# A planned order for a residual quantizer: hand-over margins and a rank offset per stage and tile

## The chip, the cores and the metric

The kernel runs on one core of one Trainium2 chip. The metric is the device time of an execution in microseconds, and the number of a kernel is the median over several executions. Before the change it is 731.85 us (six runs, 729.74 to 734.48).

## The reference

The input `x` is (2, 16000, 512) in bf16: two sequences of 16000 time steps with 512 channels. A depthwise convolution over three time steps, then SiLU, gives `z`. Four codebooks of eight vectors each then quantize it one after the other, and a second depthwise convolution makes the output.

```
z = silu(sum_i xp[:, i:i+T, :] * dw_enc[i])        # K = 3 taps
res = z; q = 0
for s in range(4):
    d2  = |res|^2 - 2 res . cb[s] + |cb[s]|^2
    idx = argmin(d2);  sel = cb[s][idx]
    q += sel;  res -= sel
y = sum_i qp[:, i:i+T, :] * dw_dec[i]              # K = 3 taps
```

The output `y` has the shape and type of `x`. The choice at each level hangs on the residual of the level before, so the levels of one row can't run side by side; different rows can.

## The kernel before

**Tiles.** The rows of the two sequences are cut into 18 tiles of G blocks of 128 rows: 6, 8, then fourteen of 16, then 8 and 6. The tensors of a tile have channels on the partitions, four blocks of 128 channels (KT = 4), so that x is loaded by transposing DMAs, one per block of rows, on SyncE (SP).

**Stages of a tile.** Each has a name in the planner's tables and these engines:

- `load`, `pad`: transposing loads into XT (two buffers), 16 to 18 for a large tile; edges by GpSimd or by two more loads.
- `taps`: three products by the encoder's weights and two sums, on half of the channels at a time (h = 0, 1), into Z. Mostly VectorE (DVE); a product may go to ScalarE (ACT).
- `exp`, `plus1`, `recip`, `gate`: SiLU as z / (1 + exp(-z)). The exponential and the reciprocal are on ACT, with a table load at each change between them; "plus one" is on DVE or ACT; the product is on DVE.
- `score0`: matmuls on TensorE (PE) of Z with itself and with the codebooks, into PSUM, half a tile at a time; DVE collects them.
- `decide`: for levels 0 to 2 a chain of small DVE instructions makes a one-hot choice. Between levels, PE transposes the one-hot (line 639), a copy on ACT or DVE brings it to SBUF (lines 643, 644), PE makes a correction from it (line 649), and DVE adds that to the scores (lines 617, 622). The scores of levels 1 and 2 thus don't need the updated residual.
- `win0`: PE transposes the one-hots of three levels (line 672), one copy brings them to OHW (line 678).
- `resid`: 24 updates per tile (three levels, two parities, four channel blocks). PE forms minus the chosen vectors in two PSUM banks (line 701). On DVE the update is an addition to Z (line 709). On ACT it is a copy (line 707), for which PE first adds Z itself by a product with the identity (line 700): four matmuls instead of two.
- `score3`, `decide3`, `win3`: the same for the last level.
- `back`: the decoder's convolution as matmuls of the one-hot windows with prepared weights (lines 758 to 762), copied by ACT to YB (line 766) and stored by SP (line 789).

**PSUM.** Four pairs of banks (PS); a step that `take`s banks holds them until the step that `free`s them has run.

**What sets the order.** All steps are entered in a list with their engine (or a choice of two), a cost in microseconds, the tensors read and written, and a key (stage, tile, place within the stage). `Plan.order` walks this list: it keeps for each engine the time at which it is free, and for each step the time at which its inputs are there; again and again it takes the step that could start first, and among equals the one with the lowest rank. The rank is the tile's number plus an offset and a slope of the stage (`WHEN`), each given for the first three tiles, the middle, and the last three. After a step, its users become ready at its end plus `LATENCY` of the engine (0.2 us for PE, 0.15 for DVE, 0.22 for ACT), or `AGAIN` on the same engine. `SHARE` decides which engine takes a residual update, `QUOTA` how many updates each may have under way, `SLACK` how much later ACT may end a movable step than DVE would. Where PE would stand idle, `order` puts filler matmuls (line 809, identity times MSK) in front of the next step; `product` models PE's granted clock. The steps are then issued in this order, which fixes each engine's instruction stream; at run time an engine takes its own stream in order and waits where an input isn't there.

Of the kernel before, what the change touches and what calls it, by code (L numbers as in the profile page):

```python
# [12 lines left out]
ACT = mybir.ActivationFunctionType  # L13
# [3 lines left out]
class Plan:  # L17
# [9 lines left out]
    SPAN, BUSY = 3.413, 0.5  # L27
    GATE = {"resid": (1.0, 2.0), "back": (1.0, 2.0), "win0": (0.6, 1.5), "win3": (0.6, 1.5), "score0": (0.25, 1.4), "score3": (0.25, 1.4)}

    def __init__(self, pairs, edges, share, slack, quota, when):  # L30
        self.steps, self.writer, self.readers = [], {}, {}
        self.pairs, self.edges, self.share, self.slack, self.quota, self.when = pairs, edges, share, slack, quota, when

    def add(self, engine, cost, key, fn, reads=(), writes=(), take=None, free=None, hold=None, tail=0.0, after=(), dest=None, box=None, mm=0):
        n = len(self.steps)
# [18 lines left out]

    def rank(self, s):
        w = self.when[s["k"][0]][self.part(s)]
        return w[0] + s["k"][1] + w[1] * s["k"][2]

    def product(self, t, c, share, half):

# [14 lines left out]
    def order(self):  # L75
# [8 lines left out]
        at = [0.0] * len(steps)  # L84
        clock = {e: 0.0 for e in self.LATENCY}
        waiting = {e: [] for e in clock}
        held = {e: 0 for e in clock}
        banks = [0.0] * (2 * self.pairs)
# [6 lines left out]
        def cost(s, e):  # L95
            return s["c"][e] if isinstance(s["c"], dict) else s["c"]

        def place(kind, t):
            if kind == "A":
                return min((max(banks[j], banks[j + 1], t), 0, j) for j in range(0, 2 * self.pairs, 2))  # L100
            return min((max(banks[j], t), -max(banks[j ^ 1], t), j) for j in range(2 * self.pairs))

        def load(d, t):
            return max(clock[d] - t, 0.0) + held[d] + sum(cost(steps[m], d) for m in waiting[d]
                                                        if at[m] <= t + 1.0 and (d == "DVE" or not isinstance(steps[m]["e"], tuple)))

        def many(s, dest):
            return s["mm"][dest] if isinstance(s["mm"], dict) else s["mm"]

        def late(m, t, c):  # L110

            return max(0.0, fetched - (t + c * (self.CHUNK - run) / m)) if run + m > self.CHUNK else 0.0

        def look(s, e):

            t = max(at[s["n"]], clock[e])
            if s["take"]:
                dest = s["dest"]
                if dest == "ANY":
                    full = [d for d in ("ACT", "DVE") if held[d] >= self.quota[d]]  # L120
                    if len(full) == 2:
                        return inf, None
                    if full:
                        dest = "ACT" if full[0] == "DVE" else "DVE"
                    else:
                        dest = "DVE" if load("DVE", t) + self.share[self.part(s)] < load("ACT", t) else "ACT"
                elif dest and held[dest] >= self.quota[dest]:
                    return inf, None
                kind = s["take"][0]
                t = place(kind[dest] if isinstance(kind, dict) else kind, t)[0]  # L130
                return t + late(many(s, dest), t, cost(s, dest) if s["dest"] == "ANY" else s["c"]), dest
            if isinstance(s["e"], tuple) and e == "ACT" and t + s["c"]["ACT"] > max(at[s["n"]], clock["DVE"]) + s["c"]["DVE"] + self.slack[self.part(s)]:
                return inf, None
            if s["mm"]:
                t += late(s["mm"], t, s["c"])
            return t, None

        def open_(n):
            e = steps[n]["e"]
            for e in e if isinstance(e, tuple) else (e,) if e else ():  # L140
                waiting[e].append(n)

        for s in steps:
            if not left[s["n"]]:
                open_(s["n"])
        while len(out) < len(steps):
            (t, dest), _, n, e = min(((look(steps[n], e), rank[n], n, e) for e, names in waiting.items() for n in names),
                                     key=lambda q: (q[0][0], q[1], q[2], q[3]))
            assert t < inf
            s = steps[n]  # L150
            for w in waiting.values():
                if n in w:
                    w.remove(n)
            c = cost(s, dest if s["take"] and s["dest"] == "ANY" else e)
            s["fill"] = None
            if s["mm"] and s["k"][0] != "setup":
                j = min(range(2 * self.pairs), key=lambda j: (banks[j], j))
                since = max(clock["PE"], banks[j])
                k = 0
                while t - clock["PE"] > self.AFTER and since + self.REST + self.FILL * (1 if self.full else 2) < t:  # L160
                    since = self.product(since, self.FILL, 1.0, 2.0)
                    k += 1
                if k > 0:
                    s["fill"] = (j, k)
                    run += k
                    if run > self.CHUNK:
                        run -= self.CHUNK
                        fetched = t + self.FETCH
            if s["take"]:
                kind, box = s["take"]  # L170
                kind = kind[dest] if isinstance(kind, dict) else kind
                j = place(kind, t)[2]
                box["banks"] = [j, j + 1] if kind == "A" else [j]
                for j in box["banks"]:
                    banks[j] = inf
                box["dest"] = dest
                if s["dest"] == "ANY":
                    steps[n + 1]["e"] = dest
                if dest:
                    held[dest] += 1  # L180
            elif s["box"] is not None:
                s["box"]["dest"] = e
            if s["hold"] and table != s["hold"]:
                table = s["hold"]
                c += self.TABLE
            if s["mm"]:
                m = many(s, dest)
                c = self.product(t, c, *self.GATE.get(s["k"][0], (0.5, 1.5))) - t
                run += m
                if run > self.CHUNK:  # L190
                    run -= self.CHUNK
                    fetched = t + c * (m - run) / m + self.FETCH
            s["t"], s["d"], s["on"] = t, c, e
            clock[e] = t + c
            self.busy[e] += c
            end = t + c + s["tail"]
            if s["free"]:
                if s["free"]["dest"]:
                    held[s["free"]["dest"]] -= 1
                for j in s["free"]["banks"]:  # L200
                    banks[j] = end + self.LATENCY[e]
            out.append(s)
            for u in users[n]:
                ue = steps[u]["e"]
                at[u] = max(at[u], t + c + self.AGAIN[e] if ue == e else end + self.LATENCY[e])
                left[u] -= 1
                if not left[u]:
                    open_(u)
# [5 lines left out]
def kernel(  # L214
# [27 lines left out]
    PAIR = 1  # L242
    NX, NE, NZ, NOH, NY = 2, 3, 4, 4, 4
    NA = 4
    SHARE = (19.5, 1.71, -1.34)
    SLACK = (0.8, -4.83, -5.72)
    QUOTA = {"ACT": 4, "DVE": 4}
    WHEN = {"setup": ((-0.05, 1.675), (0.613, 1.016), (0.464, 0.931)), "load": ((-2.074, 0.741), (-2.063, 0.601), (-2.58, 0.741)),
            "pad": ((-1.343, 0.11), (-1.736, 0.115), (-2.291, 0.134)), "taps": ((0.284, 0.643), (-0.413, 0.648), (0.441, 1.172)),
            "exp": ((0.672, 0.139), (0.624, 0.043), (0.853, 0)), "plus1": ((1.287, 0.521), (0.349, 0.234), (0.268, 0.646)),  # L250
            "recip": ((0.542, 0.819), (0.469, 0.213), (1.361, 0.627)), "gate": ((-0.104, 0.712), (0.552, 0.521), (1.523, 0.809)),
            "score0": ((-0.134, 0), (0.889, 0), (-0.19, 0)), "decide": ((1.83, 0.266), (-0.088, 0.293), (0.366, 0.69)),
            "win0": ((2.039, 0), (2.077, 0), (2.756, 0)), "resid": ((1.585, 0.742), (1.683, 0.632), (1.826, 0.993)),
            "score3": ((2.285, 1.086), (2.738, 0.327), (2.939, 1.624)), "decide3": ((1.327, 0.17), (2.815, 0.429), (3.624, 0.724)),
            "win3": ((3.135, 0.143), (3.003, 1.197), (2.818, 0.209)), "back": ((2.723, 0.576), (3.156, 1.159), (4.372, 0.628))}
    assert B == len(SIZES) and T >= GM * P and GM <= 16

    xf = x.flatten_outer_dims()
# [7 lines left out]
    tiles = []  # L266
    for b, sizes in enumerate(SIZES):
        done = 0
        for g in sizes:
            r = g * P  # L270
            t0 = max(0, min(done - 2, T - r))
            end = T if t0 + r >= T else t0 + r - 2
# [49 lines left out]
    CBN = {(s, u): sb([P, D], BF16, f"CBN{s}_{u}") for s in range(3) for u in range(2)}  # L322
    WDEC = [sb([P, D], BF16, f"WDEC{v}") for v in range(4)]

    plan = Plan(NA, (3, len(tiles) - 3), SHARE, SLACK, QUOTA, WHEN)
    add = plan.add

    def ps(box):
# [518 lines left out]
```

## Time and profile before

| | |
|---|---|
| median of six runs | 731.85 us |
| profiled execution, its own time | 730.6 us |
| its span, first to last instruction | 728.8 us |
| VectorE busy | 674.9 us (93%) |
| ScalarE busy | 658.4 us (90%) |
| TensorE busy with matmuls | 581.0 us (80%) |
| weight loads busy | 288.0 us (40%) |
| mean granted TensorE clock | 0.97 |

The rows with the largest busy time, with the mean duration of one instruction:

| line, engine, what | count | mean |
|---|---|---|
| 707 ACT, residual update, 1024 columns | 234 | 1.029 us |
| 709 DVE, residual update, 1024 columns | 102 | 1.213 us |
| 766 ACT, output copy, 1024 columns | 126 | 1.043 us |
| 537, 549 ACT, exponential and reciprocal, 4096 columns | 28 each | 3.624 us |
| 532 DVE, tap product, 2048 columns | 166 | 0.746 us |
| 364 DVE, sum or product of 4096 columns | 84 | 2.29 us |
| 539 DVE, plus one, 4096 columns | 28 | 1.218 us |

A row of the profile names the line and engine of an instruction and the tensors it writes and reads. A wait "A <- B" means that engine A stood idle before its instruction until B ended. The time of a wait is that of the waiting engine alone; whether it lengthens the kernel depends on whether the engine has other time to spare. PEclk is the granted clock of TensorE as a share of the full one. Durations are of one execution; the runs differ by some tenths of a per cent.

### The profile page before, as it was taken

The page shows a single profiled execution, that of the slowest core. Times are in us where ns is not written, and L with a number is a line of the kernel's source. Part 1 is how long each engine was busy: PE and PEld are TensorE (multiplying, and loading weights), DVE is VectorE, ACT ScalarE, POOL GpSimd, SP SyncE. Part 2 cuts the span into 40 slices and gives each one's busy share as a digit, 9 for nine tenths or more (in the row PEclk, how much of TensorE's full clock was granted, in tenths as well). Part 3 has the DMA queues.
Part 4 walks back from the last instruction along what each step waited for, and adds up shares of the span by engine and source line. Part 5 has one row for each costly group of instructions (what it writes and reads, how often), then busy time and mean ns, then how long its engine had stood idle before and what let it go on. Part 6 is the DMA issues. An engine that isn't in the chain of part 4 may idle for free.

```text
span 728.8 us, 24317 instructions
## 1 busy us (share of the span) xinstructions
PE 581.0 (80%) x10656; PEld 288.0 (40%) x10725; DVE 674.9 (93%) x1258; ACT 658.4 (90%) x583; POOL 11.3 (2%) x35
## 2 busy tenths in 40 slices
PE   4977577887898787778778877877798796889995
PEld 2433233443444443434344343433454342444442
DVE  7779889999999999999998999999999999999993
ACT  5888988599999999899998999999999999999666
POOL 2000000000010000000000000000000010000000
PEclk9999898999999999999998999989999999999999
DMA  6454545433346343645544344452535241302316
GB/s 110 99 96 96 97 109 102 118 80 74 53 128 93 117 75 102 125 94 119 96 132 88 96 118 102 142 90 57 88 119 130 71 136 24 119 2 88 117 32 212
DMA packets 163968, 71.89 MB, mean 99 GB/s; under 512 B 155567, under 2 KB 155599, under 8 KB 163862
## 3 DMA queue, kind: packets, MB, share of 16 engines
q1 hardware_dynamic: 163646, 69.90, 41.4%
q8 instruction: 84, 1.38, 0.8%
q10 hardware_dynamic: 216, 0.43, 0.3%
q14 instruction: 22, 0.18, 0.1%
HBM read 0.43 MB, written 32.77 MB: 46 GB/s over the span
## 4 chain that ended last, share of the span: by engine, by line
DVE 53%; PE 24%; issue 8%; ACT 7%; DMA 3%; SPq 3%; ACTq 0%; DVEq 0%
DVE ZB L709 12%; DVE TB L532 7%; DVE TA L364 7%; DVE ZB L364 7%; PE ps L701 6%; PE ps L700 5%; PE ps L567 5%; DVE TA L532 3%; PE ps L758 3%; DVE EX L539 2%; SPq L493 2%; PE ps L809 2%; DVE OHW L678 2%; ACT YB L766 2%; ACT EX L549 2%
## 5 line engine op out<-in xcount | busy, mean ns | idle before, releaser
L701 PE MATMUL ps<-OHW,CBN 128*128 128x512 bf16 (+1 forms) x768 | 265.1, 382 | 20.0 <-DVE ZB L709 10.6
L707 ACT CAST ZB<-ps 128x1024 bf16<-128x1024 f32 (+2 forms) x296 | 253.7, 932 | 29.7 <-PE ps L701 28.5
L700 PE MATMUL ps<-ZB,IDENT 128*128 128x512 bf16 (+1 forms) x530 | 203.2, 383 | 32.5 <-ACT ZB L707 13.6
L709 DVE TENSOR_TENSOR ZB<-ZB,ps 128x1024 bf16<-128x1024 bf16 (+2 forms) x136 | 142.8, 1062 | 2.2 <-PE ps L701 1.7
L766 ACT CAST YB<-ps 128x1024 bf16<-128x1024 f32 x126 | 121.7, 1043 | 9.9 <-PE ps L758 3.8
L701 PEld LDWEIGHTS <-CBN 128*128 128x128 bf16 x768 | 74.1, 98 | 140.5 <-issue 73.0
L537 ACT ACTIVATE EX<-ZB 128x4096 bf16<-128x4096 bf16 (+2 forms) x36 | 115.1, 3197 | 8.8 <-DVE ZB L364 8.5
L549 ACT ACTIVATE EX<-EX 128x4096 bf16<-128x4096 bf16 (+2 forms) x36 | 114.8, 3195 | 0.2
L567 PEld LDWEIGHTS <-ZB 128*32 128x32 bf16 x8064 | 75.4, 95 | 55.2 <-issue 52.2
L567 PE MATMUL ps<-ZB 128*32 128x64 bf16 x8064 | 87.5, 198 | 8.8 <-issue 5.7
L532 DVE TENSOR_SCALAR TB<-XT,WENC 128x2048 bf16<-128x2048 bf16 (+2 forms) x139 | 92.5, 683 | 0.2
L809 PE MATMUL ps<-MSK,IDENT 128*128 128x512 bf16 x277 | 71.6, 406 | 15.4 <-issue 3.1
L758 PE MATMUL ps<-WDEC,OHW 128*128 128x512 bf16 x219 | 67.4, 383 | 14.7 <-DVE ZB L709 4.8
L700 PEld LDWEIGHTS <-IDENT 128*128 128x128 bf16 x530 | 52.3, 99 | 65.2 <-issue 11.6
L364 DVE TENSOR_TENSOR ZB<-ZB,EX 128x4096 bf16<-128x4096 bf16 (+2 forms) x36 | 72.6, 2019 | 3.7 <-ACT EX L549 3.6
L364 DVE TENSOR_TENSOR TA<-TA,TB 128x4096 bf16<-128x4096 bf16 (+2 forms) x36 | 72.7, 2020 | 1.0 <-ACT TB L531 0.6
L364 DVE TENSOR_TENSOR ZB<-TA,TB 128x4096 bf16<-128x4096 bf16 (+2 forms) x36 | 72.8, 2023 | 0.1
L809 PEld LDWEIGHTS <-IDENT 128*128 128x128 bf16 x294 | 29.1, 102 | 48.1 <-issue 20.6
L532 DVE TENSOR_SCALAR TA<-XT,WENC 128x2048 bf16<-128x2048 bf16 (+2 forms) x70 | 46.7, 687 | 0.9 <-DMA XT<-in_x_dram 0.4
L758 PEld LDWEIGHTS <-OHW 128*128 128x128 bf16 x252 | 22.8, 98 | 41.9 <-issue 19.0
L539 DVE TENSOR_SCALAR EX<-EX 128x4096 bf16<-128x4096 bf16 (+2 forms) x35 | 38.4, 1096 | 0.8 <-ACT EX L537 0.8
L678 DVE COPY OHW<-ps 96x1024 bf16<-96x1024 bf16 (+5 forms) x35 | 22.1, 630 | 10.7 <-PE ps L672 5.6
(100 smaller groups left out, 396.0 us busy)
## 6 DMA issues: line engine op xcount, KB each, us to landing
out_dram<-YB SPq DMA_DIRECT2D x33, 448.0 KB
out_dram<-YB SPq DMA_DIRECT2D x28, 512.0 KB
XT<-in_x_dram SPq DMA_TRANSPOSE x283
out_dram<-YB SPq DMA_DIRECT2D x30, 60.0 KB
out_dram<-YB SPq DMA_DIRECT2D x31, 2.0 KB
out_dram<-YB SPq DMA_DIRECT2D x2, 224.0 KB
YB<-in_dw_dec_dram ACTq DMA_DIRECT2D x1, 384.0 KB
out_dram<-YB SPq DMA_DIRECT2D x1, 384.0 KB
```

The source lines that it names most:

```text
L364: add("DVE", cost, key, lambda: nc.vector.tensor_tensor(out=out, in0=a, in1=b, op=op), reads, writes, **kw)
L532: lambda dst=dst, src=src, w=w: nc.vector.tensor_scalar(out=dst, in0=src, scalar1=w, scalar2=None, op0=ALU.mult),
L537: add("ACT", act(2 * R), ("exp", n, h), lambda: nc.scalar.activation(v(ex), Z, ACT.Exp, scale=-1.0), zt, [("EX", sl), "ACTTAB"], hold="E")
L549: nc.scalar.add_instruction(mybir.InstActivation(name=nc.get_next_instruction_name(), engine=mybir.EngineType.Activation, func=ACT.Reciprocal,
L567: nc.tensor.matmul(o[HB * q:HB * (q + 1), u * ZW:(u + 1) * ZW].rearrange("p (s c) -> p s c", s=2), lhsT=blk, rhs=both, start=False, stop=( ...
L700: nc.tensor.matmul(o, lhsT=IDENT, rhs=zg[:, k0:k0 + nk, :], start=True, stop=False)
L701: nc.tensor.matmul(o, lhsT=CBN[s, u][:, i * P:(i + 1) * P], rhs=W[:, k0:k0 + nk, PADC:PADC + P], start=not on_act, stop=True)
L707: nc.scalar.copy(zg, v)
L709: nc.vector.tensor_tensor(out=zg, in0=zg, in1=v, op=ALU.add)
L758: nc.tensor.matmul(o, lhsT=W[:, k, PADC:PADC + P], rhs=WDEC[u], start=True, stop=not wrap)
L766: add("ACT", act_psum(1024), key, lambda k=k, box=box, Y=Y, k0=k0: nc.scalar.copy(Y[:, 2 * (k - k0):2 * (k - k0) + 2, :].rearrange("p g d ...
L809: nc.tensor.matmul(PS[j // 2][:, 512 * (j % 2):512 * (j % 2) + NMK * ZW], lhsT=IDENT, rhs=MSK.rearrange("p u w -> p (u w)"), start=True, s ...
```

## The change

The planner gets four margins, and every number that steers it is replaced. `MARGIN[0]` (0.11 us) is added where a step of another engine uses what PE made, `MARGIN[1]` (0.10 us) where PE uses what another engine made, `MARGIN[2]` (0.09 us) before a PSUM bank counts as free again, and PE's cost is multiplied by `MARGIN[3]` (0.99). A table `NUDGE` gives for each stage and tile an offset that is added to the rank, and, under "share" and "slack", offsets for the two choices of engine. `SHARE`, `SLACK` and `WHEN` have new values, and DVE may have three updates under way instead of four. No step, cost, latency, buffer or instruction is edited: the kernel computes the same through a different order, with some steps on the other engine and other filler.

```diff
@@ class Plan
-    def __init__(self, pairs, edges, share, slack, quota, when):
+    def __init__(self, pairs, edges, share, slack, quota, margin, when, nudge):
...
     def rank(self, s):
         w = self.when[s["k"][0]][self.part(s)]
-        return w[0] + s["k"][1] + w[1] * s["k"][2]
+        return w[0] + s["k"][1] + w[1] * s["k"][2] + self.more(s["k"][0], s)
+
+    def more(self, name, s):
+        return self.nudge.get(name, (0,) * 99)[s["k"][1]] if s["k"][0] != "setup" and s["k"][1] >= 0 else 0.0
...
-                        dest = "DVE" if load("DVE", t) + self.share[self.part(s)] < load("ACT", t) else "ACT"
+                        dest = "DVE" if load("DVE", t) + self.share[self.part(s)] + self.more("share", s) < load("ACT", t) else "ACT"
...
-            if isinstance(s["e"], tuple) and e == "ACT" and t + s["c"]["ACT"] > max(at[s["n"]], clock["DVE"]) + s["c"]["DVE"] + self.slack[self.part(s)]:
+            if isinstance(s["e"], tuple) and e == "ACT" and t + s["c"]["ACT"] > max(at[s["n"]], clock["DVE"]) + s["c"]["DVE"] + self.slack[self.part(s)] + self.more("slack", s):
...
-                c = self.product(t, c, *self.GATE.get(s["k"][0], (0.5, 1.5))) - t
+                c = self.product(t, c * self.margin[3], *self.GATE.get(s["k"][0], (0.5, 1.5))) - t
...
-                    banks[j] = end + self.LATENCY[e]
+                    banks[j] = end + self.LATENCY[e] + self.margin[2]
...
-                at[u] = max(at[u], t + c + self.AGAIN[e] if ue == e else end + self.LATENCY[e])
+                at[u] = max(at[u], t + c + self.AGAIN[e] if ue == e else end + self.LATENCY[e] + (self.margin[0] if e == "PE" else self.margin[1] if ue == "PE" else 0.0))
@@ kernel
-    SHARE = (19.5, 1.71, -1.34)
-    SLACK = (0.8, -4.83, -5.72)
-    QUOTA = {"ACT": 4, "DVE": 4}
+    SHARE = (17.22, 2.23, -0.62)
+    SLACK = (0.55, -4.13, -4.58)
+    QUOTA = {"ACT": 4, "DVE": 3}
+    MARGIN = (0.11, 0.1, 0.09, 0.99)
-    WHEN = {...
-            "win0": ((2.039, 0), (2.077, 0), (2.756, 0)), "resid": ((1.585, 0.742), (1.683, 0.632), (1.826, 0.993)),
-            "win3": ((3.135, 0.143), (3.003, 1.197), (2.818, 0.209)), "back": ((2.723, 0.576), (3.156, 1.159), (4.372, 0.628))}
+    WHEN = {...
+            "win0": ((1.053, 0.009), (1.534, 0), (2.184, 0.009)), "resid": ((1.521, 0.757), (1.683, 0.63), (1.77, 0.949)),
+            "win3": ((3.13, 0.271), (3.063, 1.197), (3.78, 0.216)), "back": ((2.796, 0.565), (3.449, 1.148), (4.298, 0.724))}
+    NUDGE = {...
+             "gate": (0.01, 0, -0.3, 0, 0.05, 0.12, 0.09, 0, 0, -0.03, 0, 0, 0, 0, -0.5, 0, 0.04, 0.08),
+             "score0": (0, 0, 0, 0, 0.56, 0, 0, 0, 0, -0.01, 0.03, -0.21, 0, 0, 0, 0, 0.04, 0.12),
...
+             "share": (0.4, -2.4, 0, -0.5, 0, 0, 0, 0, 0, 0, 0, 0, 0, 0, -1.5, -0.4, -0.4, -0.9),
+             "slack": (0.1, 0, 0, 0, 1.3, -2.8, 0, 0, 0, 0, 0, 0, 0, 0, 0, 1.4, 4, 1.2)}
```

## The prediction

> **What bounds the kernel now.** I read first the busy shares, then a table by stage, then the waits of VectorE (DVE) and ScalarE (ACT), and last the order of time in one bad stretch. The page's first part:
>
> ```profile
> PE 581.0 (80%) x10656; PEld 288.0 (40%) x10725; DVE 674.9 (93%) x1258; ACT 658.4 (90%) x583; POOL 11.3 (2%) x35
> ```
>
> The span is 728.8 us, so DVE is idle 53.9 us and ACT 70.4 us. Both are close to full and share work: each of the 432 residual updates leaves PSUM through either. Where the idle time lies, from busy time in four stretches (columns: length, then PE, PEld, DVE, ACT, POOL busy):
>
> ```profile
> 0.00:140.00 140.00, 101.46 (x1369) 48.65 (x1382) 117.76 (x257) 108.75 (x135) 3.89 (x29) 0.93 0.52 104
> 140.00:420.00 280.00, 228.00 (x4307) 113.97 (x4335) 269.30 (x451) 269.48 (x211) 4.24 (x4) 0.98 0.45 99
> 420.00:700.00 280.00, 231.97 (x4679) 116.01 (x4702) 272.30 (x513) 261.83 (x216) 3.16 (x2) 0.98 0.35 92
> 700.00:728.80 28.80, 19.54 (x311) 9.33 (x311) 15.58 (x40) 18.29 (x23) 0.00 (x0) 0.96 0.40 134
> ```
>
> DVE is idle 22.2 us in the ramp (first line), 10.7 and 7.7 in the middle, 13.2 in the drain. In the middle DVE and ACT are both 94 to 97% busy, so less work helps only if both are relieved; idle time is at most what a new order can win. Who ends those waits (columns: total us, times, longest):
>
> ```profile
> DVE OHW L678 <- PE ps L672: 5.6, 4, 2.3
> DVE rr L601 <- PE ps L567: 5.1, 2, 2.8
> DVE rr L725 <- PE ps L567: 4.6, 7, 1.6
> DVE OHW L678 <- PE ps L567: 4.2, 4, 1.8
> DVE ZB L364 <- ACT EX L549: 3.6, 3, 2.4
> DVE OT L644 <- PE ps L567: 2.5, 3, 1.2
> DVE PR L622 <- PE ps L649: 2.4, 3, 1.6
> DVE ZB L709 <- PE ps L701: 1.7, 3, 0.7
> ```
>
> and the same view for ACT:
>
> ```profile
> ACT ZB L707 <- PE ps L701: 28.5, 45, 2.1
> ACT EX L537 <- DVE ZB L364: 8.5, 6, 2.4
> ACT OT L643 <- PE ps L639: 6.8, 1, 6.8
> ```
>
> Summed over all rows, DVE waits on TensorE for 30.6 us, in short pieces: the hand-overs DVE to TensorE to DVE. How one goes wrong is seen in order of time:
>
> ```profile
> 132.68 5.75 PE L809 MATMUL ps<-MSK,IDENT 128*128 128x512 bf16 x19 [1.99 <-DVE S L602]
> 135.15 0.29 DVE L364 TENSOR_TENSOR OHA<-KEY,M 128x128 bf16<-128x128 f32 x1
> 138.28 0.22 PE L639 MATMUL ps<-IDENT,OHA 128*128 128x128 bf16 x1
> 138.53 0.27 ACT L643 COPY OT<-ps 128x128 bf16<-128x128 bf16 x1 [6.79 <-PE ps L639]
> 138.85 0.50 PE L649 MATMUL ps<-BD,OT 128*128 128x128 bf16 x6 [0.35 <-ACT OT L643]
> 139.45 0.29 DVE L622 TENSOR_TENSOR PR<-ps,S 128x128 bf16<-128x128 f32 x1 [1.61 <-PE ps L649]
> ```
>
> The one-hot is ready at 135.44; its transpose starts only after 19 filler matmuls, at 138.28. ACT, whose next instruction is the copy of that transpose, stands still 6.79 us with an exponential behind it, and DVE then waits 1.61 us.
>
> **What the Trainium skill says.** "PSUM — Partial Sum Buffer", section "Engine vs sequencer instructions": the queues of ScalarE and VectorE are strict FIFO. The 6.79 us agree: the 3.62 us exponential behind the copy was not let past. "Perfetto Trace Analysis", section "Tensor Engine Instruction (MATMUL, LD_WEIGHTS)": after a matmul's shown end, which is estimated, come PSUM's acknowledgement and the spread of the semaphore. Here the gap from PE's shown end is 0.03 us (138.50 to 138.53) and 0.10 us (139.35 to 139.45), so a margin of 0.1 us per hand-over is of the size of what the page leaves unseen. "TensorE: Matmul & The Clock Gate", section "What's actually happening": after an idle window of about 3.4 us the clock falls to half. The trace agrees where TensorE is thin: the granted clock is 0.78 from 120 to 140 us and 0.97 overall.
>
> **The change part by part.** I counted instructions of both programs in the order each engine gets them. No kind of work is added or dropped but filler; all else is moved.
>
> 1. *Engine of each movable step.* On DVE: residual updates of 1024 columns 102 to 99, of 512 15 to 16, of 384 19 to 20: -3 x 1.213 + 0.681 + 0.549 = -2.4 us. "plus one" of 4096 28 to 27, of 2048 3 to 4: -1.218 + 0.684 = -0.5. One tap of 1024 fewer: -0.5. Small one-hot transposes, 3 more on DVE: +0.65. Window copies, 2 fewer net (0.697 + 0.681 + 0.412 - 0.366): -1.4. DVE in all: -4.2, so 670.7. On ACT: residual updates 234 to 237, 33 to 32, 29 to 28: 3 x 1.029 - 0.603 - 0.520 = +2.0; one tap +1.1; plus one +1.7 (3.6 for a 4096 less 1.9); window copies about +2.2 (estimated from the update rows: 1.03 + 1.03 + 0.6, less 0.47); transposes -0.85. ACT in all: +6.2, so 664.6. DVE's part pays only while DVE is the later engine; ACT's part hides in ACT's 70.4 us of idle time. If that cover is gone, it costs its full 6.2.
>
> 2. *Hand-overs, the core of the margins.* For every DVE to TensorE to DVE hand-over I took the DVE work that stands in DVE's queue between the releasing and the collecting instruction, from the row means less 0.09 us each (three updates of 0.681 us take 1.88 us together), and compared it with what TensorE needs: 0.8 us for a one-hot transpose (690.83 to 691.61 in order of time) or its correction, and, estimated likewise, 1.1 and 1.6 for window transposes, 1.5 for a residual update, 2.0 for a score half. Missing cover, before to after: transposes 2.44 to 0.72 us, corrections 0.34 to 1.52, residual updates 0.60 to 0.00 (least cover 1.24 to 1.76; those under 3 us 19 to 9), windows 4.84 to 3.15, scores 5.00 to 4.57. Sum 13.2 to 10.0. Scaling the waits shown by it: one-hot copies (4.6 us of waits) -3.2; residual -1.7; windows (10.2) -3.5; scores (9.7) -0.9; corrections +1.2. The sum is -8.1. It leaves out queueing inside TensorE, and what DVE no longer waits for, ACT must keep pace with. I take half, -4; the bounds are -12 (three tenths of the 40.6 us that ramp and middle leave idle on DVE) and +8 (a score or window behind a longer residual run; such single waits are 2 to 3 us today).
>
> 3. *Filler.* 294 to 252 in the program. Before the first score 86 to 87, so later ones 208 to 165; on tiles 1 and 2 102 to 60, on 3 and 4 7 to 30. 25 took 5.78 us, so 43 fewer are about 10 us of TensorE, which is not the bound: 0. The cover is TensorE's own idle time; without it a burst delays a transpose as at 132.68. Bounds -2 to +2, the latter by a colder clock.
>
> 4. *ACT's queue.* One-hot copies on ACT 4 to 1, the one left on tile 0, so the 6.79 us stall goes. Output copies come in 64 runs of mean 1.97 instead of 45 of 2.80, between residual updates: TensorE needs four matmuls for a residual update through ACT and two for an output copy, so the mix should ease ACT's 28.5 us of waits. This must pay for the +6.2 and for the shorter span; no further gain counted.
>
> 5. *SyncE.* Stores now stand inside runs of loads; a store that waits for ACT's output copy holds the transposing loads behind it (about 1.27 us each to issue, 2.8 to land). After the last such store the taps are, in DVE work, 18 us or more away for tiles 8 to 17 with 2 to 13 loads left (5 to 20 us needed): hidden. Tile 6 is tight: 18 loads need 26.2 us against 25.8. Nothing counted; if the cover is gone, 0 to 4.
>
> 6. *Drain.* The last orders (15 back, 16 back, 17 back on ACT; score, decide, window on DVE) are the same: 0, bounds -2 to +2.
>
> Sum: -4.2 - 4 = -8.2 us, so a profiled execution of 730.6 (span 728.8 and 1.8 around it) becomes 722.4. The median of the runs shown is 731.85, 1.25 above that execution: forecast 723.6, say 723.5.
>
> **Rivals.** *A, fuller gain (0.22):* the hand-over estimate holds in full, and the ramp's pockets close as well: -4.2 - 12 = -16, 716. For it: the ramp's 22.2 us and fewer fillers there. Against: the first tiles are paced by loads (tiles 2 to 4 have loads 1 to 2 us of DVE work ahead of their taps, in both orders). *B, ACT becomes the bound (0.20), the slow side:* tile 4 gets 21 residual updates on ACT instead of 16, just where ACT is fullest (19.1 to 19.8 of 20 us from 140 to 240 us), and plus ones, taps and windows go there too. If ACT keeps its 70.4 us of idle time, the span grows by its added work, 6.2: 738. For it: 97% ACT in that stretch. Against: the vanished 6.79 us stall alone outweighs it. It decides from the point where ACT sheds less than 6.2 us of idle time. *C, nothing nets (0.06):* the corrections' lost cover and tile 6's loads eat part 1: within 729.7 to 734. My own case (0.52) spans 718 to 729.
>
> **How the numbers follow.** The predicted time is my own case, 723.5. A measurement can tell about 0.3% (2.2 us) from no change. Faster: A and mine, 0.74; same 0.06; slower 0.20. The range leaves a tenth on each side: below, the extremes of A; above, half of B. 713 to 737; the likeliest case alone has 718 to 729.
>
> **What would show it.** Right: DVE busy about 671 and ACT about 665; DVE's waits on TensorE near 26 us; no ACT wait on a one-hot transpose above 1 us; fewer than 22 us of DVE idle in the ramp; residual updates on DVE waiting for nothing. Wrong: ACT idle still near 70, DVE waiting for ACT's reciprocals or for input loads at tile 6, larger waits at the corrections (lines of PR and RC), or a colder clock between 120 and 250 us.

## The result, and the profile after

The changed kernel takes 736.0 us (median of 17 runs, 732.7 to 738.9), beside 732.4 us for the kernel before (38 runs on the same chips). The ratio is 1.0053 with a 95% interval of 1.0038 to 1.0068: slower by half a per cent, where 8 us less were forecast. The profiled execution has a span of 733.6 us (before 728.8) and a mean granted TensorE clock of 0.95 (before 0.97).

The busy shares of the page, for the kernel after:

```profile
PE 582.9 (79%) x10605; PEld 286.8 (39%) x10687; DVE 671.8 (92%) x1257; ACT 664.5 (91%) x584; POOL 11.3 (2%) x35
```

Busy time is what the first step of the prediction said: DVE -3.1 us, ACT +6.1. So the loss is idle time. DVE is idle for 61.8 us instead of 53.9. Where, from the busy time by stretch (length, then PE, PEld, DVE, ACT, POOL, clock, DMA share, GB/s):

```profile
0.00:140.00 140.00, 97.41 (x1131) 45.50 (x1141) 120.24 (x263) 115.27 (x138) 3.87 (x29) 0.93 0.50 102
140.00:420.00 280.00, 228.50 (x4523) 114.73 (x4556) 267.25 (x449) 268.17 (x208) 6.45 (x4) 0.95 0.47 99
420.00:700.00 280.00, 232.01 (x4565) 115.02 (x4599) 264.14 (x498) 258.57 (x213) 1.00 (x2) 0.95 0.35 87
700.00:734.00 34.00, 24.98 (x391) 11.57 (x392) 20.13 (x51) 22.50 (x28) 0.00 (x0) 0.92 0.47 160
```

DVE's idle time went from 22.2 to 19.8 us in the ramp, from 10.7 to 12.8 and from 7.7 to 15.9 in the middle, and from 13.2 to 13.4 in the drain (to the end of the span, 4.7 us later than before). Who ends DVE's waits (total us, times, longest; the lines of this kernel are those of before plus 23):

```profile
DVE ZB L732 <- PE ps L724: 9.1, 12, 3.8
DVE rr L624 <- PE ps L590: 7.9, 7, 3.0
DVE OT L667 <- PE ps L590: 3.9, 5, 1.0
DVE rr L748 <- issue: 3.6, 1, 3.6
DVE PR L645 <- PE ps L590: 2.5, 4, 1.0
DVE RC L640 <- PE ps L590: 2.2, 3, 1.2
DVE OHW L701 <- PE ps L695: 1.1, 1, 1.1
DVE OHW L701 <- PE ps L590: 1.0, 2, 0.7
```

and ACT's:

```profile
ACT ZB L730 <- PE ps L724: 33.8, 45, 3.6
ACT YB L789 <- PE ps L781: 5.7, 7, 2.8
ACT EX L560 <- DVE ZB L387: 5.6, 6, 2.3
```

Four of DVE's rows name line 590, the matmuls of the scores, as what ended a wait of OT, PR, RC or OHW. None of these reads what line 590 makes: OT copies a transposed one-hot, OHW a window of them, PR and RC add a correction. This is the clue that the experiments followed. In order of time (start, duration, engine, line, idle before and what ended it), the kernel after shows one such wait plainly:

```profile
410.84 0.63 PE L695 MATMUL ps<-IDENT,OHA 128*32 128x128 bf16 x24
412.15 0.69 PE L590 MATMUL ps<-ZB 128*32 128x64 bf16 x64
412.92 0.69 DVE L701 COPY OHW<-ps 96x1024 bf16<-96x1024 bf16 x1 [0.73 <-PE ps L590]
```

The window's transposes (line 695) end at 411.47, and DVE is free at 412.19. The copy starts at 412.92, once the score matmuls that TensorE was given after them have ended at 412.84. Window and score lie in different banks. In the program, a PSUM tile of 1024 columns is two banks, and the copy waits for the last matmul that was issued to either bank before it.

A costlier place, 12 us later:

```profile
421.98 2.28 DVE L387 TENSOR_TENSOR ZB<-ZB,EX 128x4096 bf16<-128x4096 bf16 x1
424.52 0.20 DVE L749 CAST PR<-ps 128x64 bf16<-128x64 f32 x1
424.77 0.38 PE L832 MATMUL ps<-MSK,IDENT 128*128 128x512 bf16 x1 [2.30 <-DVE PR L749]
425.37 2.77 PE L832 MATMUL ps<-MSK,IDENT 128*128 128x512 bf16 x6 [0.21 <-issue]
431.55 1.22 DVE L732 TENSOR_TENSOR ZB<-ZB,ps 128x1024 bf16<-128x1024 bf16 x1 [3.77 <-PE ps L724]
```

TensorE stands idle 2.30 us before a burst of filler. The burst writes a bank that is free; it waits because the other bank of the tile still holds a score that DVE has read only at 424.72, behind 4.56 us of sums and products. The burst then runs at half clock (its matmuls are 0.43 us apart, where others are 0.215), the score and the updates behind it come late, and DVE waits 3.77 us.

### The profile page after: what moved, and what is told of

Same layout as the page of the kernel before. It is cut to its first block, busy times and chain, and to the rows that moved or that the text cites. A ratio compares the mean times of both kernels' runs of the same rounds, so it can differ in the third digit from the quotient of the medians.

```text
span 733.6 us, 24223 instructions
## 1 busy us (share of the span) xinstructions
PE 582.9 (79%) x10605; PEld 286.8 (39%) x10687; DVE 671.8 (92%) x1257; ACT 664.5 (91%) x584; POOL 11.3 (2%) x35
## 4 chain that ended last, share of the span: by engine, by line
DVE 58%; PE 25%; issue 7%; ACT 5%; DMA 2%; SPq 2%; ACTq 0%; DVEq 0%
DVE ZB L732 12%; DVE ZB L387 11%; DVE TB L555 8%; PE ps L724 8%; PE ps L723 6%; DVE TA L387 6%; PE ps L590 5%; DVE TA L555 3%; DVE EX L562 3%; DVE OHW L701 2%; PE ps L781 2%; SPq L516 2%; DVE V L387 1%; DVE KEY L387 1%; DMA XT<-in_x_dram 1%
## 5 line engine op out<-in xcount | busy, mean ns | idle before, releaser
L730 ACT CAST ZB<-ps 128x1024 bf16<-128x1024 f32 (+2 forms) x297 | 256.4, 944 | 34.7 <-PE ps L724 33.8
L724 PE MATMUL ps<-OHW,CBN 128*128 128x512 bf16 (+1 forms) x768 | 274.9, 390 | 14.8 <-DVE ZB L732 11.2
L723 PE MATMUL ps<-ZB,IDENT 128*128 128x512 bf16 (+1 forms) x534 | 209.7, 393 | 43.2 <-ACT ZB L730 17.0
L732 DVE TENSOR_TENSOR ZB<-ZB,ps 128x1024 bf16<-128x1024 bf16 (+2 forms) x135 | 140.3, 1052 | 9.4 <-PE ps L724 9.1
L789 ACT CAST YB<-ps 128x1024 bf16<-128x1024 f32 x126 | 124.2, 1044 | 10.2 <-PE ps L781 5.7
L723 PEld LDWEIGHTS <-IDENT 128*128 128x128 bf16 x534 | 53.7, 101 | 62.2 <-issue 10.0
L832 PE MATMUL ps<-MSK,IDENT 128*128 128x512 bf16 x233 | 63.9, 417 | 16.4 <-DVE S L625 5.2
L781 PE MATMUL ps<-WDEC,OHW 128*128 128x512 bf16 x209 | 65.9, 385 | 7.4 <-DVE OHW L701 2.4
L832 PEld LDWEIGHTS <-IDENT 128*128 128x128 bf16 x252 | 25.1, 104 | 44.4 <-issue 23.0
L695 PE MATMUL ps<-IDENT,OHA 128*32 128x128 bf16 x504 | 21.1, 223 | 7.0 <-DVE S L625 2.7
```

Of the source, the lines that this page charges most:

```text
L723: nc.tensor.matmul(o, lhsT=IDENT, rhs=zg[:, k0:k0 + nk, :], start=True, stop=False)
L724: nc.tensor.matmul(o, lhsT=CBN[s, u][:, i * P:(i + 1) * P], rhs=W[:, k0:k0 + nk, PADC:PADC + P], start=not on_act, stop=True)
L730: nc.scalar.copy(zg, v)
L732: nc.vector.tensor_tensor(out=zg, in0=zg, in1=v, op=ALU.add)
L781: nc.tensor.matmul(o, lhsT=W[:, k, PADC:PADC + P], rhs=WDEC[u], start=True, stop=not wrap)
L789: add("ACT", act_psum(1024), key, lambda k=k, box=box, Y=Y, k0=k0: nc.scalar.copy(Y[:, 2 * (k - k0):2 * (k - k0) + 2, :].rearrange("p g d ...
```

## Experiments: clock, filler and place

Theories at the start: the colder clock makes the loss (C), bursts of filler stand in the way (F), or the new queue order makes the waits whatever the clock (O). Rival B of the prediction was ACT's added work. In all kernels below the outputs are computed in full.

**Less filler, in both orders.**

```diff
-            if s["fill"]:
+            if s["fill"] and s["t"] < 60.0:
                 fill(*s["fill"])
```

On the new order (137 of 252 filler matmuls left out):

> The order of the changed kernel, with all filler matmuls after the first tile's first scores left out (137 of 252). Theory C (clock): TensorE falls to half clock more often than the 15 windows between 140 and 700 us of the changed kernel, and each such window costs about 1 us: slower, 739 to 744 us. Rival F (the fillers stand in the way of needed matmuls): faster, about 730. Rival O (the new queue order makes the waits, whatever the clock): within 2 us of 736.

Measured 735.2 us, ratio to the kernel before 1.0046 (1.0028 to 1.0065).

On the old order (177 of 294 left out):

> The order of the kernel before, with all filler matmuls after the first tile's first scores left out (177 of 294). C: more half-clock windows than its 12, slower by 4 to 10 us. F: faster by 2 to 6 us. O: no change beyond 2 us.

Measured 733.9 us, ratio 1.0023 (1.0005 to 1.0042). The granted clock fell from 0.970 to 0.925, with 31 windows of 3.41 us at half clock instead of 12, for 1.7 us. The changed kernel has 21 such windows; without most of its filler it has 29 and takes no longer. So the colder clock doesn't make the 3.6 us: C falls. Filler helps the old order a little and the new one not at all. Without most of it, 1.3 us between the orders remain, but the two intervals overlap, so what part of the loss hangs on filler stays open.

**More filler, into the bank that the next step is about to write.**

```diff
             if s["fill"]:
                 fill(*s["fill"])
+            elif s["take"] and s["k"][0] != "setup" and s["t"] > 60.0 and s["idle"] > 0.1:
+                fill(s["take"][1]["banks"][0], min(8, int((s["idle"] - 0.1) / 0.22) + 1))
```

> The order of the changed kernel, with some 330 more filler matmuls from the second tile on. Each goes into the PSUM bank that the next step takes anyway, where the plan leaves TensorE idle, so that it waits for no other bank. C: the half-clock windows between 140 and 700 us fall from 15 to 5 or fewer, and the time to 727 to 732 us. F: slower by 5 us or more. O: within 2 us of 736 although the clock is up.

Measured 759.2 us, ratio 1.0366 (1.0338 to 1.0395), clock 0.974.

> The same added fillers in the order of the kernel before (some 330). C: half-clock windows between 140 and 700 us from 6 to 2 or fewer, 0 to 4 us faster than before. F: slower by 5 us or more. O: within 2 us of before, and the distance to the changed kernel's order with the same fillers stays 3 to 4 us.

Measured 764.0 us, ratio 1.0439 (1.0408 to 1.0471), clock 0.979. The clock is warmer and the kernels are 23 and 32 us slower: some 0.07 and 0.1 us for each of about 334 added matmuls. A warmer clock gains nothing here that pays for them, and TensorE's time ahead of a step counts, though TensorE is 80% busy.

**Only the bursts that wait.**

```diff
-            if s["fill"]:
+            if s["fill"] and s["n"] not in (341, 391, 488, 490, 650, 664, 682, 696, 933, 1636, 1736, 1844):
                 fill(*s["fill"])
```

> The new kernel without the 12 bursts of filler (58 matmuls of 252) whose first matmul waits for DVE or ACT to release a bank; the 16 bursts that can run at once stay. Theory F (a burst that starts late stands whole before the step behind it: 16 matmuls and 3.6 us of DVE's wait at 120.8 us, 8 matmuls and 3.8 us at 431.6 us): about 3 us less than the new kernel, 733. Theory P (the two banks of a PSUM tile share one wait, so the step behind the burst waits for the same release): 735, since only the burst's own time goes. If the later clock takes it back: 736.

Measured 735.1 us, ratio 1.0044 (1.0027 to 1.0061). F asked for 733, P for 735: the bursts are a place where the delay shows, not what makes it. (P, the theory of waits through a tile's other bank, is set out below.)

**Splices of the two orders.** For these and what follows, the planner runs with both sets of numbers, and its result is replayed: a list of step, engine and filler, in an order that `mix` gives.

```diff
-        for s in plan.order():
+        first = [s["did"] for s in plan.order()]
+        plan.share, plan.slack, plan.quota, plan.when = SHARE_B, SLACK_B, QUOTA_B, WHEN_B
+        plan.margin, plan.nudge = (0.0, 0.0, 0.0, 1.0), {}
+        other = [s["did"] for s in plan.order()]
+        for s in plan.order(mix(first, other, plan)):
```

where `mix` takes the head of one list and then, in their order, all other steps of the second.

> The first 1644 steps of the new list (to about 410 us), with their engines and filler, then all other steps in the order of the old list. Theory B (ACT's added work is what costs: the steps moved to ACT stand in tiles 0 to 4, so ahead of the cut): about 736, as the new kernel. Theory L (the loss is made by the new order of the later tiles; up to the cut the two traces are within 1 us of each other): 732, as the old one, or 1 to 2 us under it. Theory E (it is spread evenly, as a longer list of small waits): 734.

Measured 736.5 us, ratio 1.0069 (1.0042 to 1.0097).

> The reverse splice: the first 1644 steps of the old list, then the rest in the new order. Theory B: 732, as the old kernel, since the steps moved to ACT are in the other half. Theory L: 736 to 737. Theory E: 734.

Measured 744.4 us, ratio 1.0171 (1.0146 to 1.0196). No theory had this. The halves don't add up: the two splices together lose 12 us more than the two whole orders. The trace shows one place where the second one loses, just behind the seam, at the residual update of the place above:

```profile
436.75 1.22 DVE L754 TENSOR_TENSOR ZB<-ZB,ps 128x1024 bf16<-128x1024 bf16 x1 [4.63 <-PE ps L746]
```

So these two runs don't say which half makes the loss. The late splices leave less of the order to change (at the cut the lists differ by two steps, at the half splices by four):

> The old list up to its 2605th step (about 660 us), the new order for the last 45 to 75 us. The traces say that the new kernel is 3 us behind at this point and 5 us behind at 705 us, so if a loss sits in the last tiles' order: 734 to 735. If the later loss lies wholly between 410 and 660 us, or the 2 us are a delay carried from before: 732 to 733.

Measured 733.9 us, ratio 1.0024 (1.0009 to 1.0040).

> The new list up to its 2605th step, then the old order. If the last tiles' order costs 2 us: 734. If all is lost by then: 736. Theory B as the latter.

Measured 734.5 us, ratio 1.0032 (1.0014 to 1.0050). Both point to about 1.5 us of the 3.6 for the last tiles' order, but each interval is wider than that, and a splice also gives steps other banks. The rest would lie further ahead.

## Experiments: the two banks of a tile

Theory P: waits through the other bank of a tile, which the planner doesn't know. It keeps a time for each bank (`banks[j]`); the program's waits are set for whole tiles. Moreover, for a step of one bank the planner prefers the bank whose partner is taken the longest, so that whole tiles stay free:

```
return min((max(banks[j], t), -max(banks[j ^ 1], t), j) for j in range(2 * self.pairs))
```

In the two programs I compared, for each wait that goes through a PSUM tile, the banks of the waiting instruction and of the one it waits for. They differ in 93 waits of the kernel before and 119 of the kernel after. To weigh them I took the planner's own times: for each step, how long after its planned start the earlier issued steps in the other bank end (with the hand-over, and with 1 us more since the chip runs some 35 us behind its plan), summed over all that come late. This "planned lateness" is 84 us before and 143 us after. It is a scale and not a forecast. (It was reckoned anew after the first three runs below; that is why their expectations name 95, 52 and 124 us and the table further down 98 to 104, 55.7 and 114.3.)

The test keeps every engine's instructions, their order, and the filler's place and number. Only banks change. 22 steps are given a bank that the plan has free at the same time, so that the planned end moves by 0.1 us at most, and the steps behind them take theirs by the planner's rule:

```diff
-                j = place(kind, t)[2]
+                j = self.pick[n] if forced and kind != "A" and n in self.pick else place(kind, t)[2]
...
+    PICK = {257: 0, 398: 2, 488: 6, 538: 2, 541: 0, 548: 2, 615: 4, 637: 4, 701: 5, 772: 0, 970: 2, 1023: 6, 1094: 4, 1183: 0, 1501: 0, 1736: 4, 1896: 6, 1985: 3, 2056: 2, 2305: 2, 2539: 3, 2711: 4}
```

(the picks for the new order, where each burst of filler also goes to a free bank whose partner is free, if there is one).

More than 22 steps change their bank. The replay leaves out one term of the planner's times (`late`, for TensorE's steps), and for that alone it places 104 of the 704 bank-taking steps of the old order elsewhere, and 246 of the new order; with the picks for banks apart these are 308 and 359. A replay without picks was not timed. The replays of the old order have this in common and can be compared with each other; for the new order there is one replay only.

> The new kernel with each engine's instructions, their order and the filler as they are, only 22 steps put into another PSUM bank, so that waits that come from the other bank of a 1024-column tile go from 119 to 102 in the program, and the lateness of such waits by the planner's own times (all within 1 us of too late counted) from about 142 to 95 us. Theory P (this sharing, which the planner doesn't know, makes the new order's loss; old order 84 us, new 142, measured +3.6 us, so 0.06 us for each): 733. Theory O (the order of queues makes the waits, the banks don't matter): 736.

Measured 729.5 us, ratio 0.9972 (0.9959 to 0.9986): 6.5 us less than the changed kernel, and less than the kernel before.

> The same on the old kernel: 22 steps in another bank, such waits 93 to 70 in the program, their planned lateness 84 to 52 us, all else the same. Theory P: 2 us less than the old kernel, 730.5. Theory O: 732.5.

Measured 722.6 us, ratio 0.9882 (0.9854 to 0.9911). P said 2 us and it is 9.

> The reverse on the old kernel: 22 steps put where they share a tile more, such waits 93 to 101, planned lateness 84 to about 124 us, order and filler the same. Theory P: 2.5 us more than the old kernel, 735. Theory O: 732.5.

Measured 736.7 us, ratio 1.0065 (1.0044 to 1.0085). With the same instructions in the same order, O is refuted as the whole cause: the banks alone move the old order between 722.6 and 736.7 us, where Theory O gave one time for all.

In the kernel before with banks apart, the same views read (first the busy shares, then the ramp by stretch, then DVE's waits; its lines are those of before plus 46):

```profile
PE 587.0 (81%) x10725; PEld 287.3 (40%) x10725; DVE 674.7 (94%) x1258; ACT 657.5 (91%) x583; POOL 11.3 (2%) x35
```

```profile
0.00:140.00 140.00, 106.18 (x1434) 50.49 (x1435) 124.47 (x269) 114.72 (x137) 3.81 (x29) 0.96 0.52 106
140.00:420.00 280.00, 229.77 (x4372) 113.13 (x4372) 269.00 (x447) 269.18 (x213) 4.31 (x4) 0.98 0.46 101
```

```profile
DVE OHW L724 <- PE ps L718: 3.9, 4, 1.4
DVE rr L771 <- PE ps L613: 3.7, 4, 1.6
DVE rr L647 <- PE ps L613: 2.8, 2, 2.3
DVE ZB L755 <- PE ps L747: 2.4, 3, 1.0
DVE OT L690 <- PE ps L613: 1.7, 2, 1.0
DVE OHW L724 <- PE ps L613: 0.6, 1, 0.6
```

Busy time is that of before, and DVE's idle time is 46.1 us instead of 53.9. The ramp has 6.7 us more DVE work done by 140 us; the stretch behind it is as before. In the rows, one-hot and window copies that wait for the score matmuls (line 613 here, 567 before) went from 2.5 + 4.2 = 6.7 us to 2.3. In the kernel after with banks apart (lines of after plus 25) they are:

```profile
DVE OT L692 <- PE ps L615: 4.2, 6, 1.0
DVE PR L670 <- PE ps L615: 2.2, 4, 0.8
DVE ZB L757 <- PE ps L749: 8.1, 11, 2.2
ACT ZB L755 <- PE ps L749: 22.6, 43, 1.9
```

The first two rows and a window row of 0.3 make 6.7 us, where the changed kernel had 3.9 + 2.5 + 2.2 + 1.0 = 9.6. DVE's idle time is 57.5 us instead of 61.8 and ACT's 64.3 instead of 69.1. What shrank most is ACT's wait for the updates' matmuls, from 33.8 to 22.6 us (its output copies wait 6.1 us more); DVE's own, 9.1 us in the changed kernel, stays at 8.1. TensorE's own waits for DVE's small reads from PSUM (scores, one-hots, corrections, windows) are 44.2 us before, 32.9 with banks apart and 46.1 with banks shared; 55.0 after and 52.7 with banks apart. They hold needed waits as well as needless ones. With banks shared, DVE's rows of this kind don't grow (6.6 us), and TensorE's waits grow by 1.9 us alone. The profiled execution of that kernel was its shortest (732.0 us, median 736.7), so its trace does not show the whole loss.

**Equal sharing, and less still.** Is the new order the better one where both have as much of these waits? And does a further step gain?

> The old kernel with 16 of the 22 moves of before_shared: planned lateness through the other bank of a tile 101.6 us (84.2 in the old kernel, 114.3 with all 22 moves), about that of the new kernel with banks apart (98 to 104, which took 729.5). Theory P with a better new order (the change's own gain is there and is hidden by the sharing): 734.5, on the line between the old kernel and before_shared, so 5 us above the new order at equal sharing. Theory P alone (sharing explains all, the orders are worth the same): 729 to 730. Rival, a few single places rule and not the sum: 732, as the old kernel.

Measured 734.3 us, ratio 1.0027 (1.0010 to 1.0045), as P with a better new order said.

> The old kernel with 43 steps in another bank, residual updates and output copies too, and each burst of filler in a bank whose partner is free: planned lateness 50.5 us against 55.7 in before_apart (and 84.2). Theory P: 1 us less than before_apart, 721 to 722. If single places made the 9 us and they are done: 722.5.

Measured 721.2 us, ratio 0.9833 (0.9815 to 0.9852). This is the version that beats both kernels, by 1.7% and 2.2%.

| order | planned lateness, us | idle time ended through the other bank, us | ratio to the kernel before |
|---|---|---|---|
| old, banks apart, second step | 50.5 | 24 | 0.9833 |
| old, banks apart | 55.7 | 26 | 0.9882 |
| old, as it was | 84.2 | 45 | 1 |
| old, some banks shared | 101.6 | 49 | 1.0027 |
| old, banks shared | 114.3 | 53 | 1.0065 |
| new, banks apart | 98 to 104 | 51 | 0.9972 |
| new, as it was | 142.7 | 65 | 1.0053 |

The third column is measured: for each wait, the program names the awaited instruction and the trace gives its end; what is summed is the idle time of DVE, ACT and TensorE before an instruction whose last awaited one worked in the other bank of its tile and touched nothing else that it uses. It is from one execution of each. In each order the time rises with both scales, and by roughly half a microsecond for each microsecond of the third column: 13 us for 27 in the old order, 6 for 14 in the new one.

At about 100 (49 and 51 measured) the new order is 0.55% faster than the old one, 4 us. The two traces say where: DVE is busy 675.7 us in the old order with some banks shared and 671.8 in the new one with banks apart, and idle 57.3 and 57.5. The 4 us are DVE's smaller work.

**One part of the change alone.** The new planner with its margins, but with the old numbers and no rank offsets:

```diff
-    SHARE = (17.22, 2.23, -0.62)
+    SHARE = (19.5, 1.71, -1.34)
...
+    NUDGE = {}
```

> One part of the change alone: the new planner with the four margins, but with the old SHARE, SLACK, QUOTA and WHEN and no rank offsets. Its plan ends at 715.9 us against 694.9 (old) and 694.2 (new), and its program has 113 waits through the other bank of a tile against 93 and 119. If the plan's end carries over: 21 us more than the old kernel plus 2 to 3 for the sharing, 755. If the margins as such help on the chip, as the prediction had it: under 745.

Measured 748.4 us, ratio 1.0201 (1.0182 to 1.0221): between the two expectations, and 16 us slower than without margins. By themselves, on tables that were made for the old planner, the margins lose; the retuned tables bring the plan back to 694 us. DVE's waits of one-hots, corrections and windows for the score matmuls are 9.1 us there, against 7.0 in the kernel before, and by the count of the table's third column 63 us of idle time go through the other bank; so part of the 16 us may be of the same kind.

## Why the prediction was wrong

**Step 1** (engines) was right: DVE 671.8 and ACT 664.5 us busy, against 670.7 and 664.6.

**Step 2** (hand-overs) is the step that failed. It said that DVE would wait 8.1 us less for TensorE, and took half of it, 4 us. By its own classes, in us:

| class | waits before | forecast change | measured change |
|---|---|---|---|
| one-hot copies | 4.6 | -3.2 | +1.0 |
| residual updates | 1.7 | -1.7 | +7.4 |
| windows | 10.2 | -3.5 | -8.1 |
| scores | 9.7 | -0.9 | +4.5 |
| corrections | 3.4 | +1.2 | +2.8 |
| sum | 29.6 | -8.1 | +7.6 |

The sum is close to DVE's added idle time, 7.9 us. In it the scores hold the row of 3.6 us that the view puts down to "issue": the read at 120.82 starts 0.15 us after the score matmuls that it needs. The rows that name TensorE alone went from 30.2 us (the prediction summed 30.6) to 34.0.

The step measured cover between the instruction that releases a TensorE step and the one that collects it, as if a step waited for its own bank only. It left out "queueing inside TensorE" and bounded that by single waits of 2 to 3 us. What the runs showed in its place: waits go by tile, the new order has more of them (119 against 93 in the program, 65 against 45 us of idle time), and other banks for the same instructions take 6.5 us off the new order. Most of this time is TensorE's own (45 us after, 31 before). That fits the rows that grew, the waits of DVE and ACT for updates and scores; that the one makes the other is argued and not shown by itself.

The clues lay in the prediction's own fences. In the row of 4.2 us a window copy waits for line 567, and in the row of 2.5 us OT does. Both were booked as windows and one-hots; line 567 makes neither. And the stretch that ends in ACT's 6.79 us begins with 19 filler matmuls that wait 1.99 us for DVE's read of S, which lies in the other bank of the tile that the filler writes.

Two more things are wrong in the step. Its sum scales four falls to the waits shown, but takes the corrections' rise, 0.34 to 1.52 us, as it stands; scaled alike it would be 3.4 x (1.52 / 0.34 - 1) = +11.8, and the sum +2.5 instead of -8.1. And the gain of 4 us that it forecast doesn't show at equal sharing either: there the new order is 4 us faster, but DVE's idle time is the same (57.3 and 57.5 us), so that these 4 us are those of step 1. Equal values of a scale don't prove equal costs, so this is an estimate.

How far the single classes are the sharing's work is not shown. The windows fell by more than forecast; the updates' row of 9.1 us is still 8.1 with banks apart, and the scores' rows went from 14.2 us only to 13.2.

**Step 3** (filler at 0, bounds 2 us) stands: leaving out most of it took 0.8 us from the new order, within the noise, and added 1.7 to the old one. Its guess of how a burst delays a step is seen at 424.77.

**Step 4**: the 6.79 us stall of ACT is gone, as said. But ACT's waits for the updates' matmuls grew from 28.5 to 33.8 us, and the window copies that moved to ACT wait 3.0 us (1.9 for the transposes, 1.1 for DVE), so that ACT's idle time went only from 70.4 to 69.1 us and paid for next to nothing.

**Steps 5 and 6** (SyncE, drain) stand: no wait of DVE in the trace is for a load after the start, and the drain's idle time grew by 0.2 us.

**Rival B**, 738 us, had the sign, a time only 2 us off and its mark, ACT's idle time near 70. Its mechanism isn't supported: in the new order with banks apart ACT is as busy (665.0 us), and the kernel takes 729.5 us with ACT idle 64.3. The added work fits where waits are gone. Its price was not measured by itself, so as far as these runs show, the near hit is luck.

**The signs that the prediction named.** Of those of being wrong, ACT's idle time near 70 us and the larger waits at the corrections came true. Of those of being right, so did DVE's and ACT's busy time, the ramp (19.8 us of idle time) and the vanished stall; updates on DVE that wait for nothing did not.

Not settled: how much of the 3.6 us each place makes. The tail's order may have 1.5 of it, and what other banks gain is more than the difference; order and banks were not separable in the splices.

## What to carry to other kernels

When a waits row names a producer that the waiting instruction doesn't read, ask what the two share: a tile, a semaphore or a queue; here it was a PSUM tile of two banks, and naming other banks, with no instruction moved, was worth 1.7%, more than three times the whole change of order. A planner that frees buffers finer than the program's waits makes plans that the chip can't follow, and two plans that end within 1 us of each other (694.9 and 694.2 us by the planner) don't say which is faster. Before counting a gain by chains, class the waits by what really ends them.

## What was not expected of the hardware

TensorE at half clock is cheap here. Without most of its filler the old order has 19 more half-clock windows of 3.41 us and takes 1.7 us more, 0.09 us for each, and the new order has 8 more and takes no longer (735.2 us against 736.0). Both are net of the time that the missing filler gives back to TensorE. The Trainium skill ("TensorE: Matmul & The Clock Gate", "What's actually happening") gives the halving itself, and the trace agrees: matmuls of 512 columns are 0.43 us apart instead of 0.215. Added TensorE work is dear, though TensorE is not the busiest engine: about 334 matmuls of 512 columns, 0.215 us apart at full clock, cost 0.07 to 0.1 us each when they stand ahead of a step that DVE or ACT will need.
